# Three of four head groups of the wo product moved into the attention's last quarter, and both pairs of MLP chunks by seven block products

## The chip, the cores and the metric

The kernel runs on one core of a Trainium2 chip. The metric is the device time of one execution in microseconds (us); the time before is a median of three runs. Engines are named as in the profile: PE multiplies matrices (PEld loads its weights), DVE, ACT and POOL work on vectors, SP issues the DMAs. Each of them takes its instructions in order.

## The reference

`x` is 2048 tokens by 512. Cut to what is computed:

```python
xn = layernorm(x)
# attention: 32 heads of 16, each query sees itself and the 255 keys before it
q, k, v = split(xn @ wqkv)
p = softmax(where(mask, q @ k.T * 16 ** -0.5, -1e9))
s = (p @ v) @ wo                         # wo: 512 x 512
# MLP of the normalised tokens, hidden size 1792
y = layernorm(xn)                        # a second time
g = silu(gelu(y @ w1 + b1) @ w2 + b2)
out = x + s * g
```

All of it is float32.

## The kernel before

**Products.** Each float32 product is made of three passes (`PASSES`) over a high and a low part of both operands: a cast gives the high part (`split`, `settle`), a subtraction the low part. A matmul is 128 deep and, in the MLP, 128x512 in its result.

**Attention.** The heads are taken in eight quads n, the keys in 16 blocks kb. One loop, `for t in range(-16, end + 1)`, runs over t = 16n + kb up to 128; what I call a turn is one value of t. A turn makes the scores of a key block in two halves (`prob_block`: PE into `stb`, ACT takes the exponential, POOL masks), the scores of the query block 12 turns ahead for the row maxima (`max_block`, only while t < 116: PE into the one tile `xy`, DVE a predicated copy and a `tensor_reduce` from it), and the PV product of the block before (`pv_step`, 24 matmuls into `zo`, ACT copies the result to `oraw`). `max_rows` sends the maxima to memory and back as rows of the next quad's operand (`mT_d`, then `qk<-mT_d`).

**What fills the turns.** PE has more room than the attention needs, so other products stand between its parts. Three tables set where: `fills` (by turn and half turn, for PE), `plan` through `at(t, ...)` (in the middle of a turn) and `ends` through `behind(t, ...)` (at its end, mostly DMAs). `tandem(t0, t1, one, two)` spreads two products over turns t0 to t1, each 64 rows deep on one half of PE, into the banks `fb[0]` and `fb[1]`; their results leave by one ACT and one DVE copy. PE, DVE, ACT, POOL and SP all keep the order in which the code issues; SP only until the end of the attention (`nc.sync.on = False`).

Before, these fills are the Q/K and V products of later quads (`pair_qk`, `pair_v`), four transposes of the first MLP chunk's `y` (`y_turn`), and from t=99 on `pair_h`: hidden products y @ w1 of chunk 0 for ten of the 14 blocks f of the hidden size; w1 is fetched, cast and its low parts made from t=91 to 114. `first_h` makes two more at t=128.

**MLP.** The tokens are taken in four chunks c of 512. For each of the 14 blocks f there is a hidden product (12 matmuls), a gelu, a split of its result g (`split_g`), and `project`: 12 matmuls with w2 into the four accumulator banks of the chunk. Chunk 0 finds most hidden products done, chunk 1 makes all 14 (`hidden`). Chunks 2 and 3 are made together by a scheme of seven products in place of eight on 2x2 blocks (`product`; the sums of blocks of w1 are made by `combine_w`, those of y by `first_y` and `second_y`); the gelus of the second of the two chunks wait in memory (`g_d`). The y of chunks 1 to 3 is normalised and transposed by PE within the MLP. `end_chunk` adds b2 on DVE (four adds), takes four silus on ACT, multiplies the attention's result with wo (four tiles s_0 to s_3 of 128 tokens, 4 head groups of 3 passes: 12 matmuls each, into the two banks of `ps_st`), multiplies by the silu on DVE, adds x on POOL and stores. The attention's result is divided by the sum of its weights there, too (`load_o`, `split_o`).

Of the kernel before, what the change touches and what calls it, by code (L numbers as in the profile page):

```python
# [27 lines left out]
EARLY = 10  # L28
# [21 lines left out]
def mixer_kernel(ctx, tc, x, wqk, wv, wo, w1, b1, w2, b2, out):  # L50
# [8 lines left out]
    dram = ctx.enter_context(tc.tile_pool(name="dram", bufs=1, space=bass.MemoryType.DRAM))  # L59
    attn = ExitStack()  # L60
# [112 lines left out]
    wva = bigp.tile([P, 2, KT, 256], F32R, tag="wa", name="wva")  # L173
    wqs = {}
    xn_d = dram.tile([8, P, D], F32, name="xn_d")
    oT_d = dram.tile([4, 8, 32, S], F32, name="oT_d")
    rden_d = dram.tile([4, 8, S], F32, name="rden_d")
    h_d = dram.tile([EARLY - 2, P, 512], F32, name="h_d")
# [9 lines left out]
    psf = attn.enter_context(tc.tile_pool(name="psf", bufs=1, space=PSUM))  # L188
    fb = [psf.tile([P, 512], F32, name=f"fb{i}") for i in range(2)]
# [28 lines left out]
    mhalf = const.tile([P, 4], F32, name="mhalf")  # L218
# [51 lines left out]
    def split_wv_part(j):  # L270
        split(wva[:, 0, 2 * j: 2 * j + 2], wva[:, 1, 2 * j: 2 * j + 2], raws["v"][j])

    def split_wv(part=None):
        for j, raw in enumerate(raws["v"]):
            halves(wva[:, 0, 2 * j: 2 * j + 2], wva[:, 1, 2 * j: 2 * j + 2], raw, part)
# [60 lines left out]
    def job_v(hf, i):  # L336
# [3 lines left out]
        def mm(k):  # L340
            if k == 0:
                box.append(ps_st.tile([P, 2, 256], F32, tag="b", name=f"pv_{hf}_{i}"))
            j, kt, (a, b) = k // 12, k % 12 // 3, PASSES[k % 3]
            kb = 2 * i + j
            nc.tensor.matmul(box[0][:, j], big[:, a, kt, P * kb: P * (kb + 1)], wva[:, b, kt],
                             start=(k % 12 == 0), stop=(k % 12 == 11))
# [5 lines left out]
    def pair_qk(n, c):  # L352
# [11 lines left out]
        def finish(ps, t, copy):  # L364
# [17 lines left out]
            free += 2 * (t == 90)  # L382
            at(free, nc.scalar.copy, hi, raw)
            behind(free, send_high)
            free = quiet(max(free, t + 1))
# [13 lines left out]
    def pair_v(i):  # L399

        def mm(ps, k, r, **flags):
            j, kt, (a, b) = k // 12, k % 12 // 3, PASSES[k % 3]
            kb = 2 * i + j
            nc.tensor.matmul(ps[:, 256 * j: 256 * (j + 1)], big[r, a, kt, P * kb: P * (kb + 1)], wva[r, b, kt],
# [6 lines left out]
    def pair_h(f):  # L411

        def mm(ps, k, r, **flags):
            kt, (a, b) = k // 3, PASSES[k % 3]
            nc.tensor.matmul(ps, w1_part(a, f)[r, P * kt: P * (kt + 1)], mlp["yy"][b][kt][r], **flags)

        def finish(ps, t, copy):
            raw = t2.tile([P, 512], F32, tag="t2", name=f"hr_{f}")
            copy(raw, ps)
            if f < 4:  # L420
                soon[f] = raw
            else:
                behind(t, nc.sync.dma_start, h_d[f - 6], raw)
        return 3 * KT, mm, finish

    def tandem(t0, t1, one, two, mid=None, back=None):
# [18 lines left out]
        first, second = places(range(t0, mid), False), places(range(back or mid, t1), True)  # L445
# [7 lines left out]
        fills[t1, 0].append((one[2], (fb[0], t1, nc.scalar.copy)))  # L453
        fills[t1, 0].append((two[2], (fb[1], t1, nc.vector.tensor_copy)))
# [95 lines left out]
    def open_y():  # L550

        t = bigp.tile([P, 4, 512], F32, tag="wa", name="y0")
        mlp["y"] = [t[:, i] for i in range(4)]
        for i in range(4):
            nc.sync.dma_start(mlp["y"][i], xn_d[i])
        mlp["ln"] = layernorm(mlp["y"], "C0", False)
# [5 lines left out]
    W1_AREA = {6: 6, 7: 8, 8: 10, 9: 12, 10: 14, 11: 1, 12: 3, 13: 5, 2: 7, 3: 9, 0: 11, 1: 13, 4: 15}  # L562

    def open_yy():
        yh = bigp.tile([P, 2, 512], F32R, tag="wb0", name="yh")
        mlp["yy"] = ([yh[:, 0], yh[:, 1], area(4)[:, 0:512], area(4)[:, 512:1024]],
                     [area(j)[:, 512 * k: 512 * (k + 1)] for j in (0, 2) for k in range(2)])

    def open_w1():
        mlp["w1"] = bigp.tile([P, 2 * 512], F32R, tag="wb1", name="w1_5")  # L570

    def w1_part(a, f):
        at = area(W1_AREA[f]) if f in W1_AREA else mlp["w1"]
        return at[:, 512 * a: 512 * (a + 1)]
# [8 lines left out]
    def w_part(kind, a, f):  # L583
        return {"w1": w1_part, "w2": w2_part, "wo": lambda a, f: wos[:, a, f]}[kind](a, f)
# [6 lines left out]
    def fetch(kind, f):  # L591

        nc.sync.dma_start(w_part(kind, 1, f).bitcast(F32), w_d[kind][:, 512 * f: 512 * (f + 1)])
# [12 lines left out]
    def y_transpose(c, kt, ps=None):  # L606
        ts = mlp["y"]
        if ps is None:
            ps = ps_yt.tile([P, 512], F32, tag="b", name=f"yt_{c}_{kt}")
        for i in range(4):  # L610
            nc.tensor.transpose(ps[:, P * i: P * (i + 1)], ts[i][:, P * kt: P * (kt + 1)], ident)
        split(mlp["yy"][0][kt], mlp["yy"][1][kt], ps)

    def hidden_mm(ps, f, k):
        kt, (a, b) = k // 3, PASSES[k % 3]
        nc.tensor.matmul(ps, w1_part(a, f)[:, P * kt: P * (kt + 1)], mlp["yy"][b][kt],
                         start=(k == 0), stop=(k == 3 * KT - 1))

    def y_turn(kt):
# [3 lines left out]
        split(mlp["yy"][0][kt], mlp["yy"][1][kt], fb[kt % 2])  # L623
# [48 lines left out]
    for j, raw in enumerate(raws["v"]):  # L672
        nc.vector.tensor_copy(wva[:, 0, 2 * j: 2 * j + 2], raw)
        nc.gpsimd.tensor_tensor(wva[:, 1, 2 * j: 2 * j + 2], raw, wva[:, 0, 2 * j: 2 * j + 2].bitcast(F32),
                                op=ALU.subtract)
# [17 lines left out]
    for i in range(8):  # L693
# [562 lines left out]
```

## Time and profile before

| what | value |
| --- | --- |
| median of three runs | 767.04 us (766.91 to 767.17) |
| the profiled execution | 767.48 us |
| its span, first to last instruction | 765.8 us |
| busy: PE, DVE, ACT, POOL | 745.3, 526.4, 437.3, 292.3 us |
| mean granted clock of PE | 1.00 |
| HBM read and written | 51.39 and 29.62 MB |

The span is the time between the first and the last instruction that the profiler recorded; the 1.7 us around it belong to the launch. The last PV step ends at 443.8 us, the first `project` starts at 446.8 us, so the attention takes some 58% of the span and the MLP the rest. A row of a group gives the line, the engine, the operation, output and inputs by the program's names, how many there were, then their busy time and mean length, then the idle time of the engine just before them. Names such as `xnT` and `w` name the memory that a tile lies in: `xnT` is the area of the normalised tokens, parts of which are later used for weights and for y.

### The profile page before, as it was taken

What the parts mean: (1) busy time and instruction counts of PE and PEld (TensorE: products, weight loads), DVE (VectorE), ACT (ScalarE), POOL (GpSimd) and SP (SyncE); (2) the same over time, 40 slices, a digit from 0 to 9 for tenths busy, and PEclk for the clock granted to TensorE, in tenths of its full rate; (3) what the DMA queues carried; (4) which work ended last, traced back from release to release, by engine and by line L of the source; (5) the groups of instructions that cost most, each with busy time, mean ns of one, the idle gap of its engine ahead of it and who ended that gap; (6) DMA issues with size and microseconds to landing.
All of it is one profiled execution on the core that took longest, in us unless ns stands there. A gap on an engine that the chain in (4) does not pass through costs nothing.

```text
span 765.8 us, 18809 instructions
## 1 busy us (share of the span) xinstructions
PE 745.3 (97%) x7428; PEld 581.8 (76%) x7428; DVE 526.4 (69%) x833; ACT 437.3 (57%) x742; POOL 292.3 (38%) x595
## 2 busy tenths in 40 slices
PE   9899999999999999999999999999999999999997
PEld 8777676766768887676676688888878888888886
DVE  6786776877777778887874447753657665676373
ACT  7736767867666676777877755444644553442001
POOL 7612566666565554766766700030101100001102
PEclk9999999999999999999999999999999999999999
DMA  7723455656447863555735283541202322253531
GB/s 261 208 45 75 94 128 137 155 116 134 98 98 219 248 204 98 117 143 145 197 114 155 59 293 120 178 152 56 69 28 93 100 92 81 77 163 115 177 96 55
DMA packets 56951, 99.40 MB, mean 130 GB/s; under 512 B 11104, under 2 KB 11360, under 8 KB 56864
## 3 DMA queue, kind: packets, MB, share of 16 engines
q1 hardware_dynamic: 56864, 98.21, 45.2%
q8 instruction: 58, 0.95, 0.5%
q14 instruction: 29, 0.24, 0.1%
HBM read 51.39 MB, written 29.62 MB: 106 GB/s over the span
## 4 chain that ended last, share of the span: by engine, by line
PE 87%; ACT 4%; DVE 4%; issue 2%; POOL 2%; DMA 1%; SPq 0%; DVEq 0%; ACTq 0%; POOLq 0%
PE acc L42 19%; PE fb L42 18%; PE zo L42 13%; PE p L42 9%; PE stb L42 8%; PE h L42 6%; PE s L42 6%; PE xy L42 5%; ACT pt L42 3%; PE pv L42 2%; DMA x<-in_x_dram 1%; DVE xy L42 1%; DVE mt L42 1%; POOL pt L42 1%; PE yt L42 1%
## 5 line engine op out<-in xcount | busy, mean ns | idle before, releaser
L42 POOL TENSOR_SCALAR_AFFINE_SELECT pt<-pt 128x256 f32<-128x256 f32 x480 | 192.8, 426 | 161.5 <-ACT pt L42 160.4
L42 ACT ACTIVATE pt<-stb 128x768 f32<-128x768 f32 (+1 forms) x244 | 188.6, 773 | 55.5 <-PE stb L42 46.1
L42 DVE TENSOR_REDUCE mt<-xy 128x4 f32<-128x1024 f32 (+1 forms) x128 | 152.6, 1192 | 4.4
L42 PE MATMUL acc<-w,gh 128*128 128x512 f32 x432 | 134.6, 393 | 0.0
L42 DVE COPY_PREDICATED xy<-upper,zo 128x512 f32<-128x512 int32 x112 | 77.5, 692 | 69.1 <-PE zo L42 68.4
L42 PE MATMUL fb<-xnT,wqb 64*128 64x512 f32 (+1 forms) x684 | 115.2, 404 | 0.8 <-DVE xnT L42 0.8
L42 PE MATMUL zo<-pt,vt 128*17 128x128 f32 x2880 | 103.9, 275 | 1.8 <-DVE xy L42 1.3
L42 PE MATMUL stb<-qk 64*128 64x384 f32 (+1 forms) x488 | 96.7, 392 | 7.4 <-ACT pt L42 5.9
L42 POOL TENSOR_TENSOR xo<-xo,gated 128x512 f32<-128x512 f32 x15 | 20.2, 1347 | 219.0 <-DVE gated L42 215.2
L42 PEld LDWEIGHTS zo<-pt,vt 128*17 128x17 f32 x2880 | 67.5, 97 | 39.0 <-issue 17.8
L42 PEld LDWEIGHTS acc<-w,gh 128*128 128x128 f32 x432 | 80.9, 188 | 17.2
L42 PEld LDWEIGHTS stb<-qk 64*128 64x128 f32 x488 | 45.5, 183 | 52.9 <-ACT pt L42 41.6
L42 PE MATMUL acc<-w,gl 128*128 128x512 f32 x216 | 84.4, 391 | 0.0
L42 PEld LDWEIGHTS fb<-xnT,wqb 64*128 64x128 f32 (+1 forms) x684 | 63.4, 186 | 7.8 <-DVE xnT L42 1.2
L42 PE MATMUL xy<-qk 64*128 64x256 f32 (+2 forms) x536 | 61.5, 303 | 2.2 <-DVE mt L42 2.0
L42 ACT COPY oraw<-zo 128x128 f32<-128x128 f32 x128 | 34.1, 266 | 40.2 <-PE zo L42 35.5
L42 PEld LDWEIGHTS xy<-qk 64*128 64x128 f32 x536 | 43.9, 185 | 13.6 <-DVE mt L42 7.1
L42 PEld LDWEIGHTS acc<-w,gl 128*128 128x128 f32 x216 | 40.5, 188 | 9.3 <-DVE gl L42 0.2
L42 ACT ACTIVATE gated<-acc 128x512 f32<-128x512 f32 x16 | 8.7, 595 | 64.8 <-DVE acc L42 64.8
L42 PE MATMUL s<-wos,ohl 128*128 128x512 f32 (+1 forms) x204 | 44.8, 378 | 0.0
L42 PEld LDWEIGHTS s<-wos,ohl 128*128 128x128 f32 x204 | 36.7, 188 | 7.1
L42 ACT COPY p<-p 128x512 f32<-128x512 f32 x21 | 12.3, 584 | 50.1 <-PE p L42 42.6
(190 smaller groups left out, 1191.2 us busy)
## 6 DMA issues: line engine op xcount, KB each, us to landing
qk<-sh SPq DMA_DIRECT2D x128, 128.0 KB
qk<-pjr SPq DMA_DIRECT2D x64, 128.0 KB
oT_d<-oraw SPq DMA_DIRECT2D x32, 256.0 KB
w_d<-in_w_dram SPq DMA_DIRECT2D x14, 512.0 KB
x<-in_x_dram SPq DMA_DIRECT2D x16, 256.0 KB
or<-oT_d SPq DMA_DIRECT2D x16, 256.0 KB
w<-rden_d SPq DMA_DIRECT2D x16, 256.0 KB
xo<-in_x_dram SPq DMA_DIRECT2D x16, 256.0 KB
```

What stands on the lines that cost most here:

```text
L42: r = issue(*args, **kwargs)
```

## The change

- The attention's end is filled with `pair_o` instead of `pair_h`: products of the attention's result with wo, for head groups 0 to 2 and 14 of the 16 tiles of 128 tokens, nine pairs of matmuls each, in seven `tandem`s from t=98 to 127. The sums go to memory (`pre_d`), come back at each chunk's end and are added on DVE. `end_chunk` multiplies only group 3 there (three matmuls a tile), and all four groups for the last two tiles.
- For this the sums of weights are inverted in the attention (`sums`, a reciprocal on DVE at t=89, 93, 97, 101), the results of groups 0 to 2 fetched, divided and split (`fetch_early`, `divide_early`, `high_early`, `low_early`), and wo split at t=93 to 97.
- Chunks 0 and 1 are made by seven block products too: `stage(c, begun)` does a pair of chunks, and runs for 0 and 2. Their sums of y and of w1 are made from t=112 on; the first two products stand at t=128, where `first_h` stood.
- y of chunks 0 and 1 is normalised and transposed in the attention (`open_y`, `y_turn`, chunk 1 on DVE at t=97 to 105) and goes to memory (`yT_d`). For chunks 2 and 3 the transposed xn is saved at t=40 to 46 (`xT_d`), its second statistics are taken again at t=3 to 15 (`stat_again`), and POOL rebuilds y from both in the first stage (`rebuild`).
- The two banks `fb` are no longer given back after the attention; they are `ps_st` from then on.

```diff
+    def pair_o(i):
+        c, tok = i // 4, slice(P * (i % 4), P * (i % 4) + P)
+        def mm(ps, k, r, **flags):
+            g, (a, b) = k // 3, PASSES[k % 3]
+            nc.tensor.matmul(ps, o_place(c, g)[a][r, tok], wo_place(g)[b][r], **flags)
+        def finish(ps, t, copy):
+            o = t2.tile([P, 512], F32, tag="t2", name=f"pre_{i}")
+            copy(o, ps)
+            behind(t, nc.sync.dma_start, pre_d[i], o)
+        return 9, mm, finish
...
-    def y_turn(kt):
+    def y_turn(c, kt):
         for i in range(4):
             nc.tensor.transpose(fb[kt % 2][:, P * i: P * (i + 1)], mlp["y"][i][:, P * kt: P * (kt + 1)], ident)
-        split(mlp["yy"][0][kt], mlp["yy"][1][kt], fb[kt % 2])
+        t = t2.tile([P, 512], F32, tag="t2", name=f"yt_{c}_{kt}") if c or kt > 1 else mlp["scratch"][kt]
+        (nc.vector.tensor_copy if kt % 2 else nc.scalar.copy)(t, fb[kt % 2])
+        behind(now[0], nc.sync.dma_start, yT_d[c, kt], t)
...
-                               ((75, 79), (80, 84)), ((85, 90), (93, 98))), 2):
+                               ((75, 79), (80, 84)), ((85, 90), (94, 97))), 2):
...
-    for f, *span in ((6, 99, 104, 102), (8, 105, 110), (10, 111, 115), (12, 116, 121, 118, 119), (2, 122, 127, 124, 125)):
-        tandem(*span[:2], pair_h(f), pair_h(f + 1), *span[2:])
+    for c, t in ((2, 1), (3, 9)):
+        behind(t, fetch_again, c)
+        for i in range(4):
+            at(t + 2 + i + i // 3, stat_again, 4 * c - 8 + i)
...
+    for k, t in enumerate((98, 102, 108, 112, 116, 120, 124)):
+        if k in (1, 2, 3):
+            spots = [3, 2, 2, 2], [0, 0, 0, 0, 3, 2, 4]
+        else:
+            spots = [3, 3, 3], [0, 0, 0, 0, 0, 5, 4] if k == 6 else [0, 0, 0, 0, 0, 3, 3, 3]
+        tandem(t, t + 3, pair_o(2 * k), pair_o(2 * k + 1),
...
+    at(94, open_y, 1)
+    for i, t in enumerate((97, 98, 99, 100, 101, 101, 102, 103, 104, 105)):
+        at(t, y_steps, i, i + 1)
...
+    for g in range(3):
+        behind(90 + g, fetch, "early", g)
+        at((93, 94, 96)[g], settle, "early", g, nc.scalar.copy)
+        at((94, 95, 97)[g], settle, "early", g, None, nc.vector)
+    for c in range(4):
+        at(87 + 4 * c, sums, c)
+    for c, g, t, t_div, t_hi, t_lo, eng in (
+            (0, 0, 90, 94, 95, 96, dve), (0, 1, 90, 95, 96, 97, dve), (0, 2, 91, 96, 97, 98, dve),
+            (1, 0, 99, 103, 104, 105, dve), (1, 1, 99, 104, 105, 106, dve), (1, 2, 100, 105, 106, 107, dve),
...
+        behind(t, fetch_early, c, g)
+        at(t_div, divide_early, c, g)
+        at(t_hi, high_early, c, g)
+        at(t_lo, low_early, c, g, eng)
...
+    for name in ("t3", "t2", "22", "t4"):
+        for kt in range(2):
+            at(16 * NQ, high_y, name, kt)
+            at(16 * NQ, low_y, name, kt, None if name[0] == "t" and (kt or name != "t4") else nc.gpsimd)
+    fills[16 * NQ, 0] = [(product, (j, fb[j])) for j in range(2)]
...
     attn.close()
+    ps_st = psf
...
+    def rebuild(j):
+        y = ring[j % 2]
+        nc.gpsimd.tensor_tensor(y[:, 0], y[:, 0], y[:, 1], op=ALU.add)
+        nc.gpsimd.tensor_tensor(y[:, 0], y[:, 0], lnb[:, 0], op=ALU.mult)
+        nc.gpsimd.tensor_tensor(y[:, 0], y[:, 0], lnb[:, 1], op=ALU.add)
+        nc.sync.dma_start(yT_d[2 + j // KT, j % KT], y[:, 0])
...
         for i in range(4):
             between(i)
...
             ps = ps_st.tile([P, 512], F32, tag="b", name=f"s_{c}_{i}")
+            early_part = 4 * c + i < AHEAD
+            gs = (3,) if early_part else (0, 1, 2, 3)
             for cols in parts:
                 k = 0
-                for g in range(4):
+                for g in gs:
                     for a, b in PASSES:
...
+            if early_part:
+                nc.vector.tensor_add(ps, ps, pre_place(c, i))
                 nc.vector.tensor_mul(gated[:, i], ps, gated[:, i])
                 nc.gpsimd.tensor_tensor(xt, xt, gated[:, i], op=ALU.add)
...
+        def between(i):
+            if i in (1, 2):
+                mine[i - 1] = split_g(c + 1, order[i - 1], gts.pop(i - 1), nc.scalar.copy)
+                fetch_g(i + 3)
...
+    stage(0, True)
+    stage(2, False)
```

How the order of instructions changes at three places. DVE at t=97 to 99, before (`mt` and `xy` are the maxima and their scores, `pjr` a Q/K product that leaves its bank):

```order
L42 COPY_PREDICATED xy<-upper,zo 128x4x128
L42 TENSOR_REDUCE mt_12_5762<-xy 128x4
L42 COPY_PREDICATED xy<-upper,zo 128x4x128
L42 TENSOR_REDUCE mt_12_5762<-xy 128x4
L42 COPY pjr_3_5873<-fb_108 128x512
L42 COPY_PREDICATED xy<-upper,zo 128x4x128
L42 TENSOR_REDUCE mt_12_5762<-xy 128x4
```

The same turns after the change, up to the reduce of t=98 (`bnC`, `mvC`: the statistics of y; `den`: the sums of weights; `scratch`: the divided results):

```order
L42 COPY_PREDICATED xy<-upper,zo 128x4x128
L42 TENSOR_REDUCE mt_12_5856<-xy 128x4
L42 COPY pjr_3_5935<-fb_111 128x512
L42 BN_STATS bnC_0_5937<-y_5758 128x6
L42 BN_AGGR mvC_5763<-bnC_0_5937 128x2
L42 TENSOR_TENSOR xnT<-xnT 128x512
L42 TENSOR_TENSOR xnT<-scratch_5542,xnT 128x512
L42 RECIPROCAL den_5815<-den_5815 96x128
L42 COPY_PREDICATED xy<-upper,zo 128x4x128
L42 TENSOR_REDUCE mt_12_5856<-xy 128x4
```

Six instructions now stand between two turns of the maxima where none stood.

PE at the end of a chunk whose successor is already waiting, before (chunk 2; the first rows of the next chunk's `project` follow):

```order
L42 MATMUL s_2_9346<-wos,ohl_3_9253 128x512 x3
L42 MATMUL s_3_9364<-wos,ohl_0_9140 128x512 x3
L42 MATMUL s_3_9364<-wos,ohl_1_9143 128x512 x3
L42 MATMUL s_3_9364<-wos,ohl_2_9250 128x512 x3
L42 MATMUL s_3_9364<-wos,ohl_3_9253 128x512 x3
L42 MATMUL acc_0_9380<-w_0_6609,gh_0_9314 128x512 x2
```

The same place after:

```order
L42 MATMUL s_0_9545<-wos,ohl_3_9500 128x512 x3
L42 MATMUL s_1_9561<-wos,ohl_3_9500 128x512 x3
L42 MATMUL s_2_9577<-wos,ohl_3_9500 128x512 x3
L42 MATMUL s_3_9587<-wos,ohl_3_9500 128x512 x3
L42 MATMUL acc_0_9595<-w_0_7431,gh_0_9553 128x512 x2
```

Each tile has gone from twelve matmuls to three, so all four tiles now have as many as one had.

SP from t=90 on, before, between two stores of row maxima into the next quad's operand (`qk<-mT_d`):

```order
L42 DMA qk_91<-mT_d 4x2x512
L42 DMA xnT<-w_d 128x512 x3
L42 DMA mT_d<-mT_1_5551 4x32x32
L42 DMA oT_d<-oraw_8_5447 4x32x512
L42 DMA qk_706<-qk_706 4x2x512
L42 DMA qk_706<-sh_0_5474 32x2x512 x4
L42 DMA qk_706<-pjr_0_5475 32x2x512 x2
L42 DMA qk_91<-mT_d 4x2x512
```

And after, the first part of the same stretch:

```order
L42 DMA qk_94<-mT_d 4x2x512
L42 DMA rden_d<-den_5379 24x4x128
L42 DMA xnT<-wo_d 128x512
L42 DMA xnT<-oT_d 128x1x512
L42 DMA xnT<-rden_d 128x1x512
L42 DMA xnT<-oT_d 128x1x512
L42 DMA xnT<-rden_d 128x1x512
L42 DMA den_5588<-oT_d 32x1x128 x3
L42 DMA xnT<-wo_d 128x512
L42 DMA xnT<-oT_d 128x1x512
L42 DMA xnT<-rden_d 128x1x512
L42 DMA qk_719<-qk_719 4x2x512
```

Fetches of wo, of results and of reciprocals now stand ahead of the next quad's operands and of the next row maxima.

More of the change, by code (lines that the diff above doesn't have):

```diff
@@ L270, in split_wv_part @@
     def split_wv_part(j):
[L271 to L275, printed above, removed]
+        if not j:
+            wvs[1] = bigp.tile([P, 2, KT, 256], F32R, tag="wa", name="wva1")
+        split(wvs[1][:, 0, 2 * j: 2 * j + 2], wvs[1][:, 1, 2 * j: 2 * j + 2], raws["v"][j])
     stage = {}
@@ L604, in y_steps @@
         run(mlp["ln"][a:b])
[L606 to L617, printed above, removed]
@@ L847, in fetch_sums @@
[L847 to L851 removed]
+    gated = cp.tile([P, 4, 512], F32, name="gated")
+    lnb = cp.tile([P, 2, 512], F32, name="lnb")
+    open_w2(1)
+    open_w2(0)
+    for f in (7, 0):
+        fetch("w2", f)
+    ring = [bigp.tile([P, 2, 512], F32, tag=f"wb{k}", name=f"ring{k}") for k in range(2)]
```

748 lines of the change are left out of this document (366 added, 382 removed).

## The prediction

> **What bounds the kernel now.** I read the page first (busy shares, then the slices), then the tail of the chain that ended last, then stretches by window, then the costs of single instructions.
>
> ```profile
> PE 745.3 (97%) x7428; PEld 581.8 (76%) x7428; DVE 526.4 (69%) x833; ACT 437.3 (57%) x742; POOL 292.3 (38%) x595
> ...
> PE   9899999999999999999999999999999999999997
> ...
> DVE  6786776877777778887874447753657665676373
> ...
> PEclk9999999999999999999999999999999999999999
> ```
>
> PE is the bound in every slice, at full clock. DVE is at seven or eight tenths until the middle of the span and drops to four where the scores for the maxima end.
>
> ```profile
> core 0: us, PE busy (x) PEld busy (x) DVE busy (x) ACT busy (x) POOL busy (x), PEclk, DMA share, GB/s
> 355.02:387.10 32.08, 31.07 (x454) 21.31 (x452) 26.25 (x34) 26.14 (x45) 25.86 (x52) 1.00 0.69 188
> ...
> 414.59:439.25 24.66, 24.33 (x395) 16.98 (x393) 8.55 (x13) 18.72 (x34) 18.61 (x41) 1.00 0.30 88
> 439.25:761.20 321.95, 321.44 (x1486) 264.46 (x1482) 197.34 (x354) 130.31 (x216) 26.82 (x22) 1.00 0.36 114
> ```
>
> I cut the windows at the ends of PV steps: the first holds t=97 to 107 (11 turns of 2.92 us), the second t=117 to 127, the third the last PV step and the MLP. In the first PE is busy 31.07 of 32.08 us, but DVE already 26.25: it has 5.8 us to give. In the MLP PE waits 0.5 us in 322.
>
> **The MLP's work on PE.** The chain there is PE alone:
>
> ```profile
> 440.10 2.94 PE fb L42 x12
> ...
> 460.41 30.30 PE acc L42 x132
> 490.71 0.87 PE yt L42 x8
> ...
> 503.39 8.20 PE h L42 x36
> ...
> 584.70 10.89 PE s L42 x48
> 595.59 19.08 PE p L42 x84
> ...
> 711.62 38.47 PE acc L42 x168
> 750.09 11.09 PE s L42 x60
> ```
>
> One 512-wide matmul takes 19.08/84 = 0.227 us (block product), 10.89/48 = 0.227 (wo), 38.47/168 = 0.229 (w2), 8.20/36 = 0.228 (hidden); 8 transposes take 0.87.
> Before, by the loops: 672 w2, 294 block, 216 hidden (24 in `first_h`, 24 for f 4 and 5, 168 for chunk 1) and 192 wo, 1374 in all, and 48 transposes: 154.0 + 66.7 + 49.1 + 43.6 + 5.2 = 318.6 us.
> After: 672 w2, 588 block, and for wo 14 tiles of 3 and two of 12, 66 in all: 154.0 + 133.4 + 15.0 = 302.4. That is 1326 matmuls and no transposes. With the stalls of before (1.7 us), which go with the transposes on the chain, the MLP gains **18.0 us** if PE stays fed.
>
> **The price at the chunk ends.** wo's 48 matmuls were also cover. At chunk 2's end:
>
> ```profile
> 699.39 2.81 DVE L42 TENSOR_TENSOR acc<-acc,b2s 128x512 f32<-128x512 f32 x4 [0.92 <-PE acc L42]
> ...
> 700.56 11.05 PE L42 MATMUL s<-wos,ohl 128*128 128x512 f32 x48
> 700.86 1.09 ACT L42 ACTIVATE gated<-acc 128x512 f32<-128x512 f32 x2 [8.33 <-DVE acc L42]
> 702.29 1.08 ACT L42 ACTIVATE gated<-acc 128x512 f32<-128x512 f32 x2 [0.34 <-DVE acc L42]
> 703.57 0.69 DVE L42 TENSOR_TENSOR gated<-s,gated 128x512 f32<-128x512 f32 x1 [1.37 <-PE s L42]
> ...
> 711.46 0.63 PE L42 MATMUL acc<-w,gh 128*128 128x512 f32 x2
> ```
>
> Let T be the first wo matmul, 700.56. The four adds of b2 end at T+1.6, the silus at T+2.8; PE works until T+10.9 and never sees them. After, each tile has three matmuls (0.68 us), and `ps_st` still has two banks: s_2 waits until DVE has added `pre` to s_0 and multiplied, s_3 likewise for s_1. DVE: adds to T+1.6, `pre` add and multiply of tile 0 (0.69 each) to T+3.0; then the low part of g for the next chunk, which waits for its ACT cast behind the silus (2.8 + 0.62 = 3.4) and ends at T+4.1; add and multiply of tile 1 to T+5.5. So s_2 runs from 3.0, s_3 from 5.5 to 6.2, and the next chunk's w2 starts at about T+6.5, where 12 matmuls would have ended at 2.7: 3.8 us lost, at chunks 0 and 2. At chunk 1 there is no split between, s_3 starts at 4.4, and the next block product waits for s_2's bank (its multiply ends at 5.8): 3.3. At chunk 3, s_2 begins at 3.0 instead of 1.4: 1.6, and 0.3 for the adds behind the last multiplies. Sum **+12.8**; bounds 7 (split earlier than I place it) and 16.
>
> [...]
>
> **The step into the MLP.** At t=128 ACT has eight casts of `high_y` before it may empty the two banks of `product`, POOL four lows, and SP holds the second w2 fetch behind them.
>
> ```profile
> L42 ACT CAST xnT<-xnT 128x512 fp32r<-128x512 f32 x13 | 7.9, 610 | 0.0
> ...
> L42 POOL TENSOR_TENSOR xnT<-xnT 128x512 fp32r<-128x512 f32 x7 | 9.0, 1279 | 0.0
> ```
>
> ACT needs 8 x 0.61 = 4.9 us, POOL 4 x 1.28 = 5.1; PE has 24 matmuls (5.4 us) and a PV step that don't need them. Bounds 0 and 5.1, taken in the middle, **+2.7**, since the low parts follow the casts. MLP in all: -18.0 + 12.8 + 2.7 = -2.5 us.
>
> **The attention, t=97 to 107.** Here the change puts the layernorm of y1, two reciprocals, four copies out of PSUM and six low parts on DVE, and takes low parts of w1 away.
>
> ```profile
> L42 DVE TENSOR_REDUCE mt<-xy 128x4 f32<-128x1024 f32 x120 | 147.1, 1226 | 4.1
> ...
> L42 DVE COPY_PREDICATED xy<-upper,zo 128x512 f32<-128x512 int32 x112 | 77.5, 692 | 69.1 <-PE zo L42 68.4
> ...
> L42 DVE BATCH_NORM_STATS2 bnC<-y 128x6 f32<-128x512 f32 x20 | 13.3, 667 | 0.6 <-ACT y L42 0.6
> ...
> L42 DVE TENSOR_SCALAR y<-y,mvC,rsC 128x512 f32<-128x512 f32 x8 | 5.0, 646 | 0.0
> ...
> L42 DVE RECIPROCAL den<-den 128x128 f32<-128x128 f32 x4 | 3.8, 949 | 3.1 <-DMA den<-oT_d 3.1
> L42 DVE BATCH_NORM_AGGREGATE mvC<-bnC 128x2 f32<-128x6 f32 x20 | 3.6, 182 | 0.7
> ...
> L42 DVE COPY hr<-fb 128x512 f32<-128x512 f32 x5 | 3.4, 685 | 17.2 <-PE fb L42 11.9 <-POOL pt L42 5.2
> ```
>
> In the window itself (groups of DVE in t=97 to 107, then the spread of such low parts between t=0 and the end of the scores):
>
> ```profile
> L42 DVE COPY_PREDICATED xy<-upper,zo 128x512 f32<-128x512 int32 x9 | 6.2, 690 | 4.1 <-PE zo L42 4.1
> L42 DVE TENSOR_TENSOR xnT<-xnT 128x512 fp32r<-128x512 f32 x3 | 3.5, 1170 | 0.0
> ```
> ```profile
> L42 DVE TENSOR_TENSOR xnT<-xnT x6: 682/856/1353, 353.1 to 399.9; 128x512 fp32r<-128x512 f32 x6
> ```
>
> Out: three lows (3.5) and one copy (0.7): 26.25 - 4.2 = 22.05. In: statistics 4 x (0.667 + 0.182) = 3.4; four scalings 2.6; two reciprocals 1.9; four copies 2.7; six lows at 0.96 (the mean of all such) = 5.8. Together 16.4: 38.4 us of DVE in a stretch of 32.1. PE cannot pass it: its scores of turn t+1 go into the one `xy` that the reduce of turn t still reads, and the new work stands on DVE's queue between a reduce and the next copy. So +6.3, and three turns (t=100, 102, 104) have only 1.92 + 0.65 = 2.6 us on DVE where PE's turn takes 2.92, another +1: **+7.5**. Lower bound +5 (lows at their least, 0.68, and no waits); upper +10.5 (6.3 and the 4.1 that DVE waited for PE). PE's own work is equal there: nine pairs of Q/K products go earlier, sixteen transposes (1.7 us) come.
>
> [...]
>
> **The rest of the attention.** t=117 to 127: ACT gets 11 casts and copies and loses one (10 x 0.61 = 6.1 on 18.72: 24.8 in 24.66), PE six pairs of 64-row products more (at about one matmul's 0.227 each, 1.4 us): +1.5 (0 to 4). t=3 to 15: eight statistics of 0.85 in DVE's slack: +0.5 (0 to 1.5). t=89 to 96: sixteen transposes were there before; settling wo and the products' earlier end: +1 (0 to 2). Then SP's queue from t=90 on:
>
> ```profile
> 351.16 0.55 SPq L42 DMA_DIRECT2D qk<-mT_d  x1
> ...
> 353.82 2.49 SPq L42 DMA_DIRECT2D qk<-sh  x4
> ...
> 357.07 0.55 SPq L42 DMA_DIRECT2D oT_d<-oraw  x1
> 360.53 1.20 SPq L42 DMA_DIRECT2D qk<-pjr  x2
> ```
>
> The row maxima of quad 6's second chunk (`qk<-mT_d`, 351.16) go out some 7 us before t=98 reads them. 13 new DMAs and seven that used to follow now stand ahead of them, at 2.49/4 = 0.62 us an issue 12.5 us of queue; SP has gaps, such as the 2.9 us before 360.53, to catch up in. I put the issue near 357, just in time, and what it delays overlaps with DVE's delay: 0 (0 to 6). The stores of `pre_d`, `xT_d` and `yT_d` wait behind nothing on PE's path; their cover is the DMA share of 0.3 to 0.7. Attention in all +10.5.
>
> **Sum.** The profiled execution took 767.48 us (span 765.8 and 1.7 around it), 0.44 over the median of 767.04. 767.48 + 10.5 - 2.5 = 775.5, in terms of the median **775 us**. Slower by 1%; 0.2% (1.5 us) is about what a measurement can tell.
>
> **Rivals.**
> 1. Faster: the stalls at the chunk ends don't form. Place: DVE between the adds and s_3. If the split of g and the `pre` adds slip behind, each end costs 1 us and not 3 to 4, and the MLP gains 18.0 - 3 - 2.7 = 12; with +7.5 to +10.5 in the attention 764 to 767, and where DVE also hides half of its load, 759. It decides once attention and chunk ends together cost under 18. For it: 5.8 us of DVE slack, and waits of PE on DVE of only 0.3 us in the window. Against: the order of the queues. 0.18.
> 2. SP's queue sets t=93 to 101: rows of maxima late by the full 6 us, and ACT waiting for wo: 781 to 788. For it the 0.6 us of each issue; against it SP's idle stretches. 0.12.
> 3. No change: 18 us given back exactly, 767 give or take 1.5. 0.07.
> 4. [...] Rows show only 1.00: 0.05.
> 5. The forecast, 769 to 781: 0.58.
>
> Slower holds 0.75. The range takes in the bounds: low, 5 in the attention and -13 in the MLP, 759; high, +16 and +5, 788.
>
> **What would show it.** Right: in t=97 to 107 PE idle on DVE's reduce or copy with DVE over 90% busy; window of some 39 us; at each chunk end PE idle in two pieces between wo matmuls, released by DVE; the block products at 0.227 still. Wrong: if that stretch stays at 32 us, or chunk ends take under 4 us, or PE waits for a DMA there, or PEclk falls below 9.

## The result, and the profile after

The changed kernel takes 830.76 us (median of 4 runs, 827.92 to 833.09) against 767.11 (766.91 to 767.53) for the kernel before beside it: a ratio of 1.0827 [1.0793, 1.0862]. The prediction was 775, with an upper end of 788. The sign came out as forecast, and the size did not: +63.6 us instead of +8. The profiled execution of after took 831.14 us with a span of 829.4; the spans differ by the same 63.6.

The page after, lines that answer to those shown of before:

```profile
PE 759.8 (92%) x7360; PEld 584.5 (70%) x7360; DVE 597.9 (72%) x882; ACT 459.3 (55%) x795; POOL 374.5 (45%) x647
...
PE   9899998999999999958896986999989799999897
...
PEclk9999999999999999988988997999999999999999
```

PE was at nine tenths nearly everywhere and now has holes: a small one in slice 7, deep ones in 18 (five tenths), 22 and 25 (six), smaller ones at the chunk ends (30, 32 and 38). The clock row, nothing but nines before, drops in five slices.

The same by stage, cut as in the prediction, which means where the last matmuls of a PV step start. The first row holds t=21 to 25, the second t=93 to 98, the third t=99 to 105, the fourth t=117 to 127, the fifth the last PV step and the MLP:

```profile
core 0: us, PE busy (x) PEld busy (x) DVE busy (x) ACT busy (x) POOL busy (x), PEclk, DMA share, GB/s
131.68:152.46 20.78, 16.80 (x222) 11.21 (x220) 10.88 (x16) 10.69 (x20) 9.89 (x22) 0.92 0.55 94
351.83:386.49 34.66, 24.12 (x267) 16.98 (x265) 18.52 (x27) 14.95 (x28) 13.98 (x26) 0.80 0.63 178
386.49:408.83 22.34, 20.94 (x297) 14.12 (x297) 20.72 (x34) 13.97 (x24) 16.51 (x33) 1.00 0.55 149
456.56:483.36 26.80, 26.38 (x407) 18.43 (x405) 16.12 (x26) 22.63 (x44) 21.39 (x42) 1.00 0.37 114
483.36:824.97 341.61, 318.50 (x1390) 255.36 (x1386) 241.58 (x349) 147.44 (x257) 97.23 (x68) 0.97 0.47 150
```

And the turns t=21 to 25, 93 to 98 and 99 to 105 in the kernel before:

```profile
129.07:144.23 15.16, 14.82 (x223) 10.43 (x221) 10.95 (x16) 11.01 (x20) 10.54 (x23) 1.00 0.75 178
...
343.21:360.55 17.34, 16.75 (x249) 12.09 (x248) 13.31 (x19) 13.22 (x26) 10.00 (x20) 1.00 0.52 133
360.55:381.51 20.96, 20.05 (x294) 13.55 (x292) 18.72 (x26) 17.19 (x30) 16.43 (x36) 1.00 0.67 180
```

Turn by turn the attention lost 44.1 us: 2.6 up to t=20, 5.6 in t=21 to 25 (15.16 to 20.78), 0.4 in t=26 to 92, **17.3 in t=93 to 98** (17.34 to 34.66), 1.4 in t=99 to 105, **5.9 at t=106**, 1.2 in t=107 to 112, **6.9 at t=113**, and 2.7 after that, 2.1 of it in t=117 to 127 (24.66 to 26.80). By kind, PE's waits in the attention grew by 26.6 us, half clock adds 12.4, and PE's own work there, at full clock, grew by 5.1. The MLP lost 19.5, and three numbers make it up: PE waits 23.1 us instead of 0.5, half clock adds 8.3, and the work at full clock shrank by 11.3.

The largest hole first. These are rows of the timelines of SP's queue, ACT, POOL and PE from t=93 to 97 (start, duration, instruction; in brackets the idle time ahead of it and what ended it):

```profile
352.95 3.08 SPq L42 DMA_DIRECT2D den<-oT_d  x3
356.08 0.45 SPq L42 DMA_DIRECT2D xnT<-wo_d  x1
...
367.93 1.06 SPq L42 DMA_DIRECT2D yT_d<-scratch  x2
...
372.86 0.55 SPq L42 DMA_DIRECT2D qk<-mT_d  x1
361.36 0.62 ACT L42 CAST xnT<-xnT 128x512 fp32r<-128x512 f32 x1 [4.58 <-DMA xnT<-wo_d]
...
372.07 0.62 ACT L42 CAST xnT<-scratch 128x512 fp32r<-128x512 f32 x1 [7.06 <-POOL scratch L42]
370.78 1.26 POOL L42 TENSOR_TENSOR scratch<-xnT 128x512 f32<-128x512 f32 x1 [13.53 <-issue]
362.62 1.48 PE L42 MATMUL zo<-pt,vt 128*17 128x128 f32 x24 [4.35 <-DVE xy L42]
...
372.45 0.63 PE L42 MATMUL zo<-pt,vt 128*17 128x128 f32 x8 [3.58 <-POOL pt L42]
```

Read it from the queue outwards. A load of wo goes out at 356.08, behind three loads of sums. ACT's next instruction is the cast of that piece, so ACT stands for 4.58 us, with the exponentials behind it. Then the division on POOL wants to write a `scratch` tile whose old content, a transposed y, is stored only at 367.93, behind a dozen transfers for Q and K. POOL waits 13.53 us (the row says "issue", since it shows no releaser; the stores went out 2 us before it went on). ACT's next cast waits 7.06 us for POOL, the causal masks stand behind the division on POOL, and PE has neither exponentials nor masks. How much of the lateness is the order of issue and how much the load of the DMA engines stays open: their busy share in this stretch is 0.63 where it was 0.52, and no run took bytes away there. The row maxima, on which the prediction had built its SP step, go out at 372.86 instead of 351.16.

t=106 and t=113 are the same thing on a smaller scale:

```profile
400.76 5.54 SPq L42 DMA_DIRECT2D qk<-sh  x4
...
428.39 5.57 SPq L42 DMA_DIRECT2D xnT<-yT_d  x4
413.44 0.69 PE L42 MATMUL stb<-qk 64*128 64x384 f32 x2 [3.76 <-DMA qk<-mT_d]
442.30 0.62 ACT L42 CAST xnT<-xnT 128x512 fp32r<-128x512 f32 x1 [5.40 <-DMA xnT<-yT_d]
443.68 0.69 PE L42 MATMUL stb<-qk 64*128 64x384 f32 x2 [5.50 <-ACT pt L42]
```

At t=106 the maxima are late by SP's queue. At t=113 ACT reaches the cast of block 21 of y, planned for t=112 although its part is used at t=119; the loads ahead of it took 5.57 us, and all of ACT waits 5.40 us.

Early in the span the statistics that `stat_again` takes are stored by two DMAs of 1024 numbers, each number on its own:

```profile
131.24 1.33 SPq L42 DMA_DIRECT2D ln_d<-ln  x2
...
135.05 9.41 SPq L42 DMA_DIRECT2D qk<-sh  x4
145.85 0.62 ACT L42 CAST wva<-wvr 128x512 fp32r<-128x512 f32 x1 [2.71 <-DMA wvr<-in_wv_dram]
```

Four such issues took 2.46 us at 125.92 and take 9.41 behind these stores, and ACT waits for what lies behind.

The entry into the MLP, and a chunk end (DVE, PE and SP):

```profile
491.92 1.27 SPq L42 DMA_DIRECT2D w<-w_d  x3
497.67 0.43 DVE L42 TENSOR_TENSOR w<-w 128x256 f32<-128x256 f32 x1 [6.33 <-DMA w<-w_d]
...
501.56 0.79 PE L42 MATMUL p<-xnT 128*128 128x512 f32 x1 [6.14 <-DVE xnT L42]
...
514.59 0.77 PE L42 MATMUL p<-xnT,wh 128*128 128x512 f32 x2 [3.46 <-ACT p L42]
604.67 1.54 PE L42 MATMUL s<-wos,ohl 128*128 128x512 f32 x6
607.75 0.97 PE L42 MATMUL s<-wos,ohl 128*128 128x512 f32 x3 [1.54 <-DVE gated L42]
611.00 1.65 PE L42 MATMUL s<-wos,ohl 128*128 128x512 f32 x3 [2.29 <-DVE gated L42]
...
658.36 3.05 PE L42 MATMUL s<-wos,ohl 128*128 128x512 f32 x6 [4.19 <-DVE gated L42]
```

The chunk end at 604.67 (chunk 0) looks as the prediction drew it: six wo matmuls, an idle piece, three, a second idle piece, three, both released by DVE. The last row is chunk 1. The entry doesn't look as drawn: DVE waits 6.33 us for the second pair of w1 blocks, part of which goes out in the row at 491.92, behind a w2 fetch whose tile POOL's low parts still held.

Last, windows on three of the ten low stretches of the clock:

```profile
143.10:146.51 3.41, 3.41 (x36) 2.04 (x32) 1.84 (x3) 0.69 (x3) 0.77 (x2) 0.50 0.76 233
371.80:378.63 6.83, 6.17 (x38) 4.43 (x38) 2.52 (x3) 3.82 (x7) 4.73 (x9) 0.50 0.71 183
610.74:614.15 3.41, 3.15 (x7) 2.48 (x8) 3.34 (x6) 0.00 (x0) 2.79 (x2) 0.50 0.91 318
```

All ten are at 0.50, last 3.41 or 6.83 us and start during or just after a stall of PE. The three wo matmuls at 611.00 take 1.65 us, where the three at 607.75, at full clock, took 0.97. PE is busy in the ten stretches for 41.4 us; half of that, 20.7 us, is taken as lost, an estimate from this clock: 12.4 in the attention, 8.3 in the MLP.

### The profile page after: what moved, and what is told of

It is laid out like the page before. It is cut to its first block, busy times and chain, and to the rows that moved or that the text cites. A ratio compares the mean times of both kernels' runs of the same rounds, so it can differ in the third digit from the quotient of the medians.

```text
span 829.4 us, 19166 instructions
## 1 busy us (share of the span) xinstructions
PE 759.8 (92%) x7360; PEld 584.5 (70%) x7360; DVE 597.9 (72%) x882; ACT 459.3 (55%) x795; POOL 374.5 (45%) x647
## 5 line engine op out<-in xcount | busy, mean ns | idle before, releaser
L42 POOL TENSOR_SCALAR_AFFINE_SELECT pt<-pt 128x256 f32<-128x256 f32 x480 | 197.9, 436 | 177.5 <-ACT pt L42 175.1
L42 PE MATMUL acc<-w,gh 128*128 128x512 f32 x448 | 143.3, 401 | 0.0
L42 PE MATMUL p<-xnT,wh 128*128 128x512 f32 x380 | 119.2, 395 | 3.5 <-ACT p L42 3.5
L42 PE MATMUL fb<-xnT,wqb 64*128 64x512 f32 (+1 forms) x684 | 118.5, 417 | 0.3 <-DVE xnT L42 0.3
L42 PE MATMUL stb<-qk 64*128 64x384 f32 (+1 forms) x488 | 99.5, 402 | 20.0 <-ACT pt L42 14.0
L42 PEld LDWEIGHTS acc<-w,gh 128*128 128x128 f32 x448 | 86.2, 192 | 21.1
L42 PE MATMUL acc<-w,gl 128*128 128x512 f32 x224 | 89.7, 400 | 0.0
L42 PEld LDWEIGHTS p<-xnT,wh 128*128 128x128 f32 x380 | 72.4, 191 | 20.1 <-ACT p L42 3.9
L42 PE MATMUL p<-xnT 128*128 128x512 f32 x190 | 75.3, 396 | 6.1 <-DVE xnT L42 6.1
L42 ACT COPY p<-p 128x512 f32<-128x512 f32 x41 | 23.9, 585 | 81.3 <-PE p L42 78.8
```

The source lines that it names most:

```text
L42: r = issue(*args, **kwargs)
```

## The experiments

Each is an edit of the changed kernel; ratios are to the kernel before, run beside it (767.1 to 767.6 us).

**The stores of the statistics, moved, then reshaped.** First the two stores later:

```diff
-            behind(19, nc.sync.dma_start, ln_d[k].rearrange("(i p) -> p i", p=P), ln2_[:, k])
+            behind(62, nc.sync.dma_start, ln_d[k].rearrange("(i p) -> p i", p=P), ln2_[:, k])
```

> The two stores of the second statistics (ln_d, 1024 elements of 4 bytes each) go out at t=62 instead of t=19; nothing else changes. In the changed kernel t=22 to 24 take 14.25 us against 8.71 before, the four qk<-sh issues behind the stores 9.41 us against 2.5, and the clock is at half for 3.41 us. Queue theory (the small elements hold up what stands behind them on SP's queue, and ACT waits for wv): t=22 to 24 come back to 8.7 us and the time falls by 5 to 6 us, to 824 to 826. Rival (the extra loads and statistics at t=3 to 15 are what delays that stretch): no change there, 830.

831.19 us, 1.0833 [1.0799, 1.0866]: no change. t=21 to 25 came free (t=25 ends at 146.0 instead of 152.5), and t=70 lost as much (7 us). In the timeline of PE there:

```profile
280.86 0.69 PE L42 MATMUL stb<-qk 64*128 64x384 f32 x2 [4.68 <-DMA qk<-mT_d]
```

A half clock of some 6.8 us follows (mean granted clock 0.57 from 280 to 288 us). The cost goes where the stores go; it is theirs and not that of the place. Next the same numbers, transposed on DVE and stored by one DMA in rows of 128 bytes:

```diff
-        for k in range(2):
-            behind(19, nc.sync.dma_start, ln_d[k].rearrange("(i p) -> p i", p=P), ln2_[:, k])
+        nc.vector.memset(ln2r[:, 16:32], 0.0)
+        nc.vector.transpose(lnT, ln2r)
+        behind(19, nc.sync.dma_start, ln_d.rearrange("r (i t) -> i r t", i=4), lnT)
```

> The second statistics are turned by a DVE transpose of 32x32 blocks first, so that one DMA of 128-byte runs stores them at t=19 (as max_rows does), in place of two stores of 1024 elements of 4 bytes. Moved to t=62 those stores had freed t=20 to 25 (6.5 us) and cost as much around t=67. If the small elements are what costs: t=22 to 24 at 8.7 to 9.5 us, no new gap later, and 6 to 9 us less, 822 to 825. If the store's place is what costs and not its form: no change, 830.

822.81 us, 1.0724 [1.0688, 1.076]: 8.0 us less than after. The loss of 5.6 us in t=21 to 25 is gone from the trace; the rest of the 8.0 is no more than the runs' scatter (820.6 to 826.4, and 827.9 to 833.1 for after). SP's queue:

```profile
129.75 0.55 SPq L42 DMA_DIRECT2D ln_d<-lnT  x1
...
132.65 2.49 SPq L42 DMA_DIRECT2D qk<-sh  x4
```

The issues behind the store are at 2.49 us again, and no later turn up to t=92 lost anything. The cause of this piece is shown: 2048 numbers of four bytes, stored one by one (in after's trace 2113 packets of under 512 bytes start from 131 to 135 us). With them the queue took 9.41 us for the four issues, with rows 2.49.

**The chunk ends: banks and order, or filled with unused work.**

```diff
+        between(1)
         for u in us:
             nc.vector.tensor_add(u, u, b2s)
...
-            between(i)
+            if i == 2:
+                between(i)
...
-            ps = ps_st.tile([P, 512], F32, tag="b", name=f"s_{c}_{i}")
+            ps = (ps_st if i < 2 else ps_yt).tile([P, 512], F32, tag="b", name=f"s_{c}_{i}")
```

> At the chunk ends the four tiles of wo use four banks (two of ps_yt beside the two of ps_st), and the next chunk's first g is split before the adds of b2. In the changed kernel PE idles 3.8, 4.2, 3.9 and 1.6 us there (13.5 in all) and runs 3.41 us at half clock behind each of the first three. Theory (s_2 and s_3 wait for DVE to free two banks): these gaps nearly close and the half clock with them, 13.5 less about 1 left, plus 3 x 1.7 of clock: 12 to 17 us less, 814 to 819. Rival (DVE's adds themselves are the limit, banks or not): 3 to 5 us less, 826.

812.26 us, 1.0584 [1.0568, 1.06]: 18.5 us less. All of the waits at chunks 0, 2 and 3 are gone. The tail of the chain of waits, now PE alone:

```profile
756.28 2.74 PE s L42 x12
759.02 39.35 PE acc L42 x168
```

Chunk 1 still waits 2.83 us. So the stalls were those of two banks and of DVE's order, as the prediction had them. They fell by 13.5 - 2.8 us, some 10.6, and the three half-clock stretches behind them, 5.0 us, went too; the rest of the gain lies mostly in the waits at the MLP's entry, which this edit doesn't touch and which differ between runs (8.5 us here, 9.6 in after's). Banks and order were changed together, so their shares aren't known. The other edit leaves the stalls' causes as they are and gives PE unused matmuls in the idle pieces:

```diff
+            if i in (1, 2) and c < 3:
+                if i == 1:
+                    idle = ps_yt.tile([P, 512], F32, tag="b", name=f"idle_{c}")
+                for k in range((6 if c != 1 else 15) if i == 1 else (9 if c != 1 else 0)):
+                    nc.tensor.matmul(idle, os_[3][0][:, 0:P], wos[:, 0, 3], start=True, stop=True, skip_group_check=True)
```

> PE gets matmuls whose result nobody uses into a free bank, in the idle time between the tiles of wo at three chunk ends (6 and 9 of them at chunks 0 and 2, 15 at chunk 1); nothing else changes and none of the waits is taken away. If the half clock behind each chunk end is the price of PE standing idle: it stays at full clock there and the time falls by 3 x 1.7 = 5 us, 825 to 826, with the ends themselves as long as before. If the clock falls for another reason: 830 to 832.

823.23 us, 1.0726 [1.0709, 1.0743]: 7.5 us less than after, with no useful work moved. A window on the end of chunk 0, and PE's timeline there:

```profile
604.00:614.00 10.00, 9.61 (x40) 7.54 (x41) 7.14 (x10) 1.73 (x4) 5.51 (x4) 1.00 0.85 273
```
```profile
602.44 1.52 PE L42 MATMUL idle<-wos,ohl 128*128 128x512 f32 x6
604.14 0.96 PE L42 MATMUL s<-wos,ohl 128*128 128x512 f32 x3 [0.18 <-DVE gated L42]
```

The clock stays at 1.00 where it was 0.50. Half clock had cost 5.0 us at three chunk ends (half of 3.15 + 3.35 + 3.41 us of busy PE). The rest is not the edit's: the two waits at the MLP's entry were 7.6 us in this run and 9.6 in after's, and the attention took 2.7 us less. That PE's idleness brought the half clock here is shown.

**SP's queue at t=89 to 96.** First one chosen wait, the stores that `scratch` waits for, issued at once:

```diff
-        behind(now[0], nc.sync.dma_start, yT_d[c, kt], t)
+        if c or kt > 1:
+            behind(now[0], nc.sync.dma_start, yT_d[c, kt], t)
+        else:
+            nc.sync.dma_start(yT_d[c, kt], t)
```

> Only the place of two DMAs on SP's queue changes: the first two stores of the transposed y of chunk 0 (yT_d, out of the scratch that the first divisions write to) go out in the middle of t=91, some 12 issues earlier. In the changed kernel POOL stands 13.5 us before the first division, and t=94 to 96 take 24 us against 8.3. Queue theory (POOL waits for those stores, which stand in SP's queue, and ACT and PE wait for POOL): t=95 and 96 come down by 7 to 11 us with the half clock, 820 to 823; the wait of ACT for wo at t=94 (4.6 us) stays. DVE theory (the stretch is slow because DVE is full, as the prediction had it): no more than 2 us.

828.15 us, 1.0792 [1.0776, 1.0808]: 2.6 us less, hardly more than the runs' scatter. POOL's 13.53 us are gone (it now waits 3.57, put down to a load of wo), t=96 ends 5.8 us earlier, and t=98 ends where it ended, at 386.6: ACT meets another late transfer, a piece of wo. Its timeline:

```profile
363.27 0.62 ACT L42 CAST xnT<-xnT 128x512 fp32r<-128x512 f32 x1 [5.81 <-DMA xnT<-wo_d]
```

Then that together with fewer issues on SP (the loads of xn at t=1 and 9 are merged in the same way as those of y):

```diff
-        for g in range(3):
-            nc.sync.dma_start(den[32 * g: 32 * g + 32], oT_d[g, :, DH, cols].rearrange("a (q t) -> a q t", q=4))
+        nc.sync.dma_start(den, oT_d[0:3, :, DH, cols].rearrange("g a (q t) -> (g a) q t", q=4))
...
-        for i in range(4):
-            nc.sync.dma_start(mlp["y"][i], xn_d[4 * c + i])
+        nc.sync.dma_start(t, xn_d[4 * c: 4 * c + 4].rearrange("i p d -> p i d"))
...
-        behind(90 + g, fetch, "early", g)
+        at(90, nc.scalar.dma_start, wo_place(g)[1].bitcast(F32), w_d["wo"][:, 512 * g: 512 * (g + 1)])
```

> Fewer issues on SP around t=87 to 97, the same work: the three loads of the sums of weights of a chunk become one, four loads of y one, wo's three early loads go by ACT's queue at t=90, and the first two stores of y's transpose go out at once (as in the run that moved those alone, 2.6 us faster). That is about ten of some 25 added issues at 0.6 us. Queue theory: t=94 to 98 take 32 us in the changed kernel against 11.2 before; they come down by 8 to 14 us with their half clock, 815 to 822. DVE theory: PE's time there is set by the DVE queue, 826 to 829.

823.57 us, 1.0728 [1.0692, 1.0764]: 7.2 us less, not most of the 17. In the traces t=93 to 98 lost 13.4 us instead of 17.3 and t=106 1.4 instead of 5.9, while t=113 lost 2 us more. The timeline of DVE has a new wait, for the 1 MB load that now stands for four:

```profile
379.50 0.69 DVE L42 BATCH_NORM_STATS2 bnC<-y 128x6 f32<-128x512 f32 x1 [7.46 <-DMA y<-xn_d]
```

**DVE's load.** The layernorm of y1 left out:

```diff
-    for i, t in enumerate((97, 98, 99, 100, 101, 101, 102, 103, 104, 105)):
-        at(t, y_steps, i, i + 1)
```

> Leaves out the second layernorm of chunk 1 (statistics and scaling on DVE at t=97 to 105, 6 to 6.5 us of DVE); the loads, transposes and stores stay. By the prediction's account DVE is the bound in t=97 to 107 and this gives back 4 to 6 us: 825 to 827. By the queue theory PE waits there for DMAs (t=98 and 106), DVE is rarely last, and it gives 0 to 2.5: 828 to 831.

828.19 us, 1.0779 [1.0759, 1.08]: 2.6 us less, again hardly more than the scatter. With DVE freed, PE waits at t=106 for the row maxima instead, longer than the 3.76 of after:

```profile
409.66 0.69 PE L42 MATMUL stb<-qk 64*128 64x384 f32 x2 [4.69 <-DMA qk<-mT_d]
```

**The MLP's entry and t=113.** The second pair of w1 ahead of w2's blocks, these settled later, and the casts of block 21 moved from t=112 to 116:

```diff
-        for name, t_hi, t_lo in (("21", 112, 119), ("t1", 116, 118), ("11", 124, 125)):
+        for name, t_hi, t_lo in (("21", 116, 119), ("t1", 116, 118), ("11", 124, 125)):
...
-    for f in (7, 0):
-        fetch("w2", f)
...
-                    for f in ((1, 8), (2, 9), (3, 10), (4, 11), (5, 12), (6, 13), ())[g]:
+                    for f in ((7, 0, 1, 8), (2, 9), (3, 10), (4, 11), (5, 12), (6, 13), ())[g]:
```

> Two waits on single loads are taken away: at the start of the MLP the second pair of w1 is fetched ahead of the w2 part whose place the last low parts of y still hold, and w2's first two casts move from the middle of the first group to its end; and the casts of y's block 21 move from t=112, 113 to 116, 117, four turns behind their loads. The changed kernel idles 6.1 and 3.5 us in the first two groups and 5.5 at t=113, each with half clock. If these loads are the cause: the first gap closes to 0 to 2 us, the one at t=113 to 0 to 1, 12 to 17 us less, 814 to 819. Rival (DVE and POOL are late with the low parts anyway, and the ACT work moved to t=116 is as late there): 3 to 6 us less, 825 to 827.

818.83 us, 1.0677 [1.0654, 1.0699]: 12.0 us less. The wait at t=113 is gone (6.9 us lost there before, 0.2 now), so its cause is shown: the cast stood too early. The waits at the entry shrank only by a third at most:

```profile
489.10 0.50 PE L42 MATMUL p<-xnT 128*128 128x512 f32 x1 [4.78 <-DVE xnT L42]
...
501.07 0.73 PE L42 MATMUL p<-xnT,wh 128*128 128x512 f32 x2 [2.38 <-ACT p L42]
```

So the w2 fetch was not the main thing that made the second pair of w1 late. SP's and DVE's timelines of this run, in which the first block product starts at 473.04 (in after's at 484.14, 11.1 us later):

```profile
478.56 3.06 SPq L42 DMA_DIRECT2D w<-w_d  x3
...
486.29 0.43 DVE L42 TENSOR_TENSOR w<-w 128x256 f32<-128x256 f32 x1 [6.04 <-DMA w<-w_d]
```

Counted from the first product, the load that DVE waits for goes out 2.6 us earlier than in after, and DVE goes on only 0.3 us earlier. Why it lands so late stays open.

**All repairs together.** The reshaped store, SP's relief, the chunk ends, the casts, the second statistics a turn later each, the layernorm of y1 two turns later, and the second pair of w1 loaded at t=118 into a free place:

```diff
+    behind(118, lambda: fetch_pair(1, (late(8), late(9))))
```

> The repairs together: statistics stored as rows, fewer issues on SP around t=87 to 97, casts of y's block 21 four turns later, four banks at the chunk ends, and for the start of the MLP the second pair of w1 fetched at t=118 into memory that is free by then, with w2's low half of the hidden blocks one group later. Besides, the second statistics of chunks 2 and 3 start one turn later and those of y1 two turns later. The separate runs gave 18.5, 8, 7 and 12 us. If the waits are independent: 830.8 - 45.5 = 785, less another 3 to 6 for the start of the MLP and y1, 779 to 785. If one wait hides behind another (one queue, whose lateness shows at the next place): 790 to 805. The time before, 767, would be reached only if the attention lost no more than the 18 us that the MLP's matmuls save.

800.8 us, 1.0436 [1.0419, 1.0454]. The single gains (8.0 + 18.5 + 7.2 + 12.0) would give 785. They don't add: where one wait goes, another that ran beside it is left. DVE's timeline names one, the reciprocal that waits for the sums and holds the maxima behind it:

```profile
375.94 0.95 DVE L42 RECIPROCAL den<-den 96x128 f32<-96x128 f32 x1 [6.32 <-DMA den<-oT_d]
```

So the reciprocals went to later turns, the loads of y into four pieces again, and one w2 cast to an earlier place:

```diff
-        at(91 + 4 * c - 2, invert)
+        at((89, 95, 104, 110)[c], invert)
...
-        at(87 + 4 * c, sums, c)
+        at((87, 91, 98, 106)[c], sums, c)
```

> The run of all repairs (800.8) with three waits more taken away: the reciprocals of chunks 1, 2 and 3 go from t=93, 97, 101 to t=95, 104, 110 (there DVE stood 2.5 and 6.3 us before them, waiting for the sums' load, and the scores of the maxima behind it); y's load is four DMAs again (the one of 1 MB was followed by 5.4 us in which SP issued nothing); and w2's block 0 is cast in the middle of the second group and not at its end (PE waited 3.9 us for it). If DVE's in-order wait for the sums is what holds t=93 to 98: these turns lose 6 to 9 us and 3 to 5 of half clock, the start of the MLP 3 to 5, in all 786 to 790. If the loads are late for all, and the next consumer waits in their place: 795 to 800.

792.88 us, 1.0345 [1.0322, 1.0369]: the best of these versions, and 25.8 us slower than the kernel before. Its timelines of PE and ACT still show a stop at t=98:

```profile
371.56 0.69 PE L42 MATMUL stb<-qk 64*128 64x384 f32 x2 [6.78 <-ACT oraw L42]
...
401.59 0.51 PE L42 MATMUL stb<-qk 64*128 64x384 f32 x2 [2.20 <-DMA qk<-mT_d]
371.25 0.27 ACT L42 COPY oraw<-zo 128x128 f32<-128x128 f32 x1 [5.45 <-DMA oT_d<-oraw]
```

The copy waits until the store that reads its tile has gone out, again SP's queue. t=93 to 98 take 27.8 us in this trace, still 10.5 more than in the kernel before. Two more runs from here. Without the layernorm of y1:

```diff
-    for i, t in enumerate((99, 100, 101, 102, 103, 103, 104, 104, 105, 105)):
-        at(t, y_steps, i, i + 1)
```

> The kernel of the run before this one in the list (reciprocals later), and it leaves out the second layernorm of chunk 1 as an earlier run did on the changed kernel, where that gave 2.6 us. There PE's other waits in t=94 to 106 may have hidden DVE's load. If DVE is the bound of t=98 to 107 once they are gone: 5 to 7 us less than the kernel with it. If DVE's load of t=97 to 107 costs little of itself: 1 to 3 us less.

793.04 us, 1.034 [1.0323, 1.0358]: nothing gained. And the accumulators of w2 in other PSUM banks, the last four instead of the third to sixth, by opening `ps_yt` ahead of `ps_mx`:

> The kernel with the reciprocals later (792.9), with one thing changed: the accumulators of the MLP lie in the last four of the eight PSUM banks and not in the third to sixth (before the change they lay in the first four). Every kernel with the change runs a matmul with w2 in 0.233 to 0.234 us, where the kernel before takes 0.229, at the same granted clock of 1.00; over 672 of them that is 3 us. If the place of the accumulators causes it: 0.229 again and about 3 us less, 789 to 790. If it has to do with what the operands share their memory with: 0.233 as before and 793.

795.15 us, 1.0346 [1.031, 1.0382] beside 1.0345. In the chain of waits of this run the last chunk's w2 products are

```profile
746.88 39.20 PE acc L42 x168
```

or 0.233 us each, as without the edit. This choice of banks changes nothing; the first four, where they lay in the kernel before, were not tried.

## Why the prediction was wrong, point by point

- **SP's queue, "0 (0 to 6)": the step that failed first.** It looked at one transfer, the row maxima, and asked whether they would come in time. It did not ask who waits in order for the other late ones. Each of wo, the y blocks and the stores of `scratch` has a consumer on ACT or POOL that stands ahead of exponentials and masks. t=93 to 98, 106 and 113 lost 17.3 + 5.9 + 6.9 = 30.1 us, waits and the half clock after them. At t=113 this is shown by the edit that removed it; at t=93 to 98 it is read from the traces, and the repairs together gave back 6.8 of the 17.3 us there. Rival 2 had the place and gave it 0.12, at 781 to 788; its price counted the maxima's 6 us and one wait for wo. In the two runs on single pieces of it (2.6 and 7.2 us back) another late transfer stands in the place of the one repaired.
- **t=3 to 15, "+0.5" (0 to 1.5).** It priced the eight statistics on DVE and passed over the two stores behind them, which cost 5.6 us at t=21 to 25. Up to t=20 it was 2.6 us, in other versions 1.5 to 6, so this price was low as well.
- **t=97 to 107, "+7.5" of DVE.** DVE is nearly full, as forecast: busy 20.72 of 22.34 us in t=99 to 105, 93%. But that stretch lost 1.4 us, with PE's waits on DVE under 1 us each, and taking the layernorm away gave 2.6 us in one version and 0 in another. Part of the load was never there: over t=97 to 107 DVE is busy 34.06 us, not 38.4. Five low parts at 0.72 us stand there where the sum has six at 0.96, three new copies where it has four, and one reduce of 1.2 us falls outside. The sum also let none of the new work run while PE stood for something else. The window named in the prediction would have looked right (42.89 us instead of 39) for the wrong reason: its ends take in the stalls of t=98 and 106.
- **t=117 to 127, "+1.5".** 2.1 measured; right. But PE's own work was taken as equal in the rest of the attention, and over all of it grew by 5.1 us.
- **The chunk ends, "+12.8".** The four ends measured 3.8, 4.2, 3.9 and 1.6, in all 13.5, with the releaser foretold and, at chunks 0 and 2, in the pieces. Right, and shown by exchanging the banks and the order. Chunk 1 differs in detail: one piece, since DVE's low parts for the next product stood ahead of the adds.
- **The step into the MLP, "+2.7" (0 to 5.1).** 9.6 us of waiting. It priced ACT's casts and POOL's low parts, and no load that lands late; DVE's wait for the second pair of w1 is such a load. Sending it ahead of the w2 fetch hardly helped, so the reason for its lateness is not known.
- **The MLP's work, "-16.2" of matmuls.** 11.3 measured. The block products are at 0.227 still (9.55/42), but a w2 matmul takes 39.35/168 = 0.234 instead of 0.229, 3.5 us over 672 (both from the chain of the run with the chunk ends repaired). What slows it stays open. Another 1.4 I can't assign.
- **The clock, 0.05.** The rows of before show 1.00 throughout, and no run then at hand showed what idle pieces do to the clock. The pieces at the chunk ends came as foretold; during or just after them and seven other stalls the clock fell to 0.50, ten times in all, for 20.7 us. At three chunk ends it cost 1.6 to 1.7 us each (half of 3.15, 3.35 and 3.41 us of busy PE). The sum has no such term at all; about half of it is contained in the 30.1 us above.
- **Rival 1.** Its sum is off: 12 less in the MLP and 7.5 to 10.5 more in the attention give 762.5 to 765.5, not 764 to 767. Nothing hangs on it.

By place this is the whole of it: 44.1 us in the attention and 19.5 in the MLP, the half clock included in each. What stays open besides is the last 25.8 us of the best repaired version (28.9 between the spans of its profiled run and before). There PE idles 25.6 us more than before, among them 6.78 us at t=98, 2.2 and 1.9 for row maxima, 6.3 at the MLP's entry and 2.9 at chunk 1; half clock adds 10.3, and PE's work is 7.0 less. Whether an order exists in which all these transfers come in time was not found.

## What to carry to other kernels

A plan that moves work into a full stretch must be read from the queue outwards: list every transfer it adds or delays, and for each the first instruction that waits for it and what stands behind that one on its engine; here the prices lay there and not in the engines' busy time. Work that is taken away was also cover (wo's products at the chunk ends), and the stalls that opened there cost half clock as well as their own length: 3.8, 4.2 and 3.9 us of waiting, and 1.6 to 1.7 us of clock behind each. When several waits run side by side, a repair of one shows little; judge by the trace where the wait went, and expect the gains of single repairs not to add.

## What the runs showed of the hardware that was not expected

- Half clock came here without an unbroken idle stretch of its own length: 3.41 us at 0.50 after 1.54 + 2.29 us with three matmuls between (chunk 0), its start in the second of the two, and 3.41 us at 0.50 after 1.04 + 1.88 us at t=22 and 23. The length of a wait alone doesn't decide: behind the wait of 2.83 us at chunk 1's end, in the run with the chunk ends repaired, the pairs of matmuls took 0.62 to 0.73 us, as at full clock; in the best version, behind a wait of 1.36 us at t=91, a PV step took 1.49 us instead of 0.85, and the mean clock was 0.88 and 0.78 in the two 5 us from 340 us on. In after each stretch lasted 3.41 or 6.83 us; in the best version the three 5 us from 365 us on had 0.77, 0.50 and 0.71, some 10.2 us at half clock in all, an estimate from these means.
- Two stores of 1024 single numbers took 1.33 us to issue, and the four issues of `qk<-sh` behind them took 9.41 us, where with the reshaped store they took 2.49.
- An issue on SP's queue is not always 0.6 us: four went out in 5.54 and 5.57 us in after, where four took 2.46 at 125.92.
